# Causal scores of a chunk in pieces of 32 key columns, placed on the four column groups of TensorE

## The chip, the cores and the metric

The kernel runs on one core of one Trainium2 chip. The metric is the device time of one execution in microseconds (us); lower is better.

PE is the matmul array, PEld its weight loads, DVE the vector engine, ACT the scalar engine, POOL the GpSimd engine, SP the engine that issues most of the loads.

## The reference

Two blocks in sequence. The first is a gated linear recurrence over tokens (4 sequences, 8 heads, 768 tokens, 48 channels a head); the second a feed-forward layer on 3072 tokens of width 384, with 1024 hidden units.

```python
for t in range(S):                       # S = 768, for each of B = 4 sequences and H = 8 heads
    S_re, S_im = ar * S_re - ai * S_im, ar * S_im + ai * S_re
    S_re = S_re + einsum('bhd,bhe->bhde', k[:, :, t], v[:, :, t])
    y[:, :, t] = einsum('bhd,bhde->bhe', q[:, :, t], S_re)
x = y as (3072, 384)
h = x @ w_in                             # 384 -> 1024
solu = h * softmax(h)
out = layernorm(solu) * g_ln @ w_out     # 1024 -> 384
```

## The kernel before

The recurrence is computed in 24 chunks of 128 tokens. In a chunk each head needs scores (keys times queries, 128 x 128), of which only those with query token >= key token count; a mask of ones and zeros (`tri`) removes the rest. The masked scores (`f_att`) then weight the values (`f_v`), and the state carried from the chunks before is added. Everything is fp32.

```python
def score(half):                          # 4 heads each
    ps = ps_s.tile([P, 4, P], FP, tag="s", name="f_score")
    for i in range(4):
        x = half * 4 + i
        nc.tensor.matmul(out=ps[:, i], lhsT=KT[:, x * P:(x + 1) * P], rhs=QT[:, x * P:(x + 1) * P],
                         start=True, stop=True)
    nc.vector.tensor_tensor(out=st["att"][:, half * 4:half * 4 + 4], in0=ps,
                            in1=tri.unsqueeze(1).to_broadcast([P, 4, P]), op=OP.mult)

def values():
    V = T["v", g][:, own]
    ...
    for x in range(H):
        hs = slice(x * D, (x + 1) * D)
        for r in range(0, P, 32):         # four column groups: output partitions r..r+31
            nc.tensor.matmul(out=y[r:r + 32, hs], lhsT=st["att"][:, x, r:r + 32], rhs=V[:, hs], ...)
        ...                               # the same with qT and the carried state
```

The `values` step (`f_y`) and the carry (`f_d`, which updates the state) already use weights of 32 columns, written to output partitions 0, 32, 64 and 96, that is, to the four column groups of the array. The scores use all 128 columns at once. One iteration of the main loop, cut to the order that matters (the loop works on three chunks at a time, and every second iteration differs in the gate work):

```python
for n in range(2, N + 2):
    score(0); score(1)      # f_score of chunk n
    turn_x()                # f_xt: three 128-wide transposes of chunk n-1
    down(0)                 # f_o of chunk n-2
    values()                # f_y of chunk n
    up(0)                   # f_h of chunk n-1
    turn(...)               # f_turned: transposes of q and k of chunk n+1
    up(1)
    carry()                 # f_d of chunk n
    turn(...)
    down(1)
    turn_z(0); turn_z(1)    # f_zt of chunk n-1; in every second iteration f_phase follows
```

## Time and profile before

| what | value | where from |
|---|---|---|
| median time | 555.27 us (554.70 to 555.46, 3 runs) | the times |
| span of the profiled execution | 553.1 us | the page |
| third score starts (the loop begins) | 98.96 us | starts of matmuls in the trace |
| third score to the first matmul of the last f_o stage ("the loop" from here on) | 442.34 us | the same |
| mean granted PE clock, first 100 us / 100 to 500 us | 0.80 / 1.00 | busy time by windows |

The busy time of each engine, from the page:

```profile
PE 482.6 (87%) x5604; PEld 309.4 (56%) x5604; DVE 367.3 (66%) x714; ACT 305.4 (55%) x497; POOL 17.9 (3%) x52
```

87% for PE is an average over two regimes: the first 100 us, in which PE is often idle or slow, and a loop in which it hardly stops. The prediction below shows the lines for that. An fp32 matmul appears in the trace as two passes, each with a weight load of its own.

### The profile page before, as it was taken

The page shows a single profiled execution, that of the slowest core. Times are in us where ns is not written, and L with a number is a line of the kernel's source. Part 1 is how long each engine was busy: PE and PEld are TensorE (multiplying, and loading weights), DVE is VectorE, ACT ScalarE, POOL GpSimd, SP SyncE. Part 2 cuts the span into 40 slices and gives each one's busy share as a digit, 9 for nine tenths or more (in the row PEclk, how much of TensorE's full clock was granted, in tenths as well). Part 3 has the DMA queues.
Part 4 walks back from the last instruction along what each step waited for, and adds up shares of the span by engine and source line. Part 5 has one row for each costly group of instructions (what it writes and reads, how often), then busy time and mean ns, then how long its engine had stood idle before and what let it go on. Part 6 is the DMA issues. An engine that isn't in the chain of part 4 may idle for free. (4 is left out here: it accounts for less than half of the span.)

```text
span 553.1 us, 13053 instructions
## 1 busy us (share of the span) xinstructions
PE 482.6 (87%) x5604; PEld 309.4 (56%) x5604; DVE 367.3 (66%) x714; ACT 305.4 (55%) x497; POOL 17.9 (3%) x52
## 2 busy tenths in 40 slices
PE   0265744799999999999999999999999999999994
PEld 0144323455765666666666666567567656666652
DVE  4668435957677768759759669669578677564333
ACT  4755447375656565575575665665655665642220
POOL 0000000000000000000000000000000000000000
PEclk9957786899999999999999999999999999999999
DMA  9998633431613615416316305206214000000001
GB/s 205 235 246 159 129 97 104 109 66 39 115 54 59 130 44 88 102 44 115 75 44 131 58 17 101 58 17 120 44 32 82 14 3 17 14 17 1 15 15 36
DMA packets 134243, 42.23 MB, mean 76 GB/s; under 512 B 127392, under 2 KB 130464, under 8 KB 134176
## 3 DMA queue, kind: packets, MB, share of 16 engines
q1 hardware_dynamic: 133328, 40.91, 34.6%
q8 instruction: 46, 0.75, 0.6%
q10 hardware_dynamic: 848, 0.40, 0.3%
q14 instruction: 21, 0.17, 0.1%
HBM read 36.51 MB, written 4.72 MB: 75 GB/s over the span
## 5 line engine op out<-in xcount | busy, mean ns | idle before, releaser
L866 PE MATMUL f_h<-f_w_in,f_xT 128*128 128x512 f32 x288 | 135.7, 609 | 7.5 <-ACT f_xT L861 7.5
L908 PE MATMUL f_o<-f_w_out,f_zT 128*128 128x384 f32 x384 | 133.5, 492 | 2.5 <-DVE f_w_out L645 2.5
L908 PEld LDWEIGHTS f_o<-f_w_out,f_zT 128*128 128x128 f32 x384 | 70.2, 192 | 43.1 <-DVE f_w_out L645 2.7
L866 PEld LDWEIGHTS f_h<-f_w_in,f_xT 128*128 128x128 f32 x288 | 52.0, 193 | 57.7 <-issue 48.0
L874 ACT ACTIVATE f_z<-f_h 128x512 f32<-128x512 f32 x48 | 28.6, 597 | 91.5 <-PE f_h L866 91.5
L875 DVE TENSOR_TENSOR f_z<-f_h,f_z 128x512 f32<-128x512 f32 x48 | 33.1, 689 | 47.2 <-ACT f_z L874 47.2
L813 PEld LDWEIGHTS f_score<-f_qT,f_kT 96*128 96x128 f32 x384 | 46.5, 195 | 3.0
L813 PE MATMUL f_score<-f_qT,f_kT 96*128 96x128 f32 x384 | 47.6, 278 | 0.0
L796 PE MATMUL f_turned<-f_mats,f_k 128*96 128x128 f32 x192 | 32.1, 293 | 17.8 <-DVE f_k L784 17.8
L796 PEld LDWEIGHTS f_turned<-f_mats,f_k 128*96 128x96 f32 x192 | 21.8, 132 | 34.8 <-DVE f_k L784 25.3
L884 ACT COPY f_zT<-f_zt 128x512 f32<-128x512 f32 x48 | 26.7, 587 | 26.2 <-PE f_zt L883 25.6
L831 DVE COPY f_xn<-f_y 128x384 f32<-128x384 f32 x24 | 13.2, 552 | 41.6 <-PE f_y L828 35.4
L798 ACT COPY f_kT<-f_turned 96x512 f32<-96x512 f32 x48 | 27.6, 576 | 18.1 <-PE f_turned L796 18.1
L825 PEld LDWEIGHTS f_y<-f_v,f_att 128*32 128x32 f32 x1536 | 30.4, 109 | 8.9 <-issue 7.5
L703 PE MATMUL f_L<-f_lr,f_mats 128*128 128x384 f32 x48 | 19.0, 522 | 18.5 <-DVE f_lr L696 18.5
L825 PE MATMUL f_y<-f_v,f_att 128*32 128x48 f32 x1536 | 34.0, 207 | 0.3 <-DVE f_att L815 0.3
L815 DVE TENSOR_TENSOR f_att<-f_score,f_mats 128x512 f32<-128x512 f32 x48 | 31.1, 683 | 4.3 <-PE f_score L813 4.3
L796 PE MATMUL f_turned<-f_mats,f_q 128*96 128x128 f32 x192 | 31.3, 289 | 2.7 <-DVE f_q L784 2.7
L896 DVE BATCH_NORM_STATS2 f_bs<-f_z 128x6 f32<-128x512 f32 x48 | 30.7, 680 | 0.0
L704 DVE TENSOR_SCALAR f_lr<-f_L 128x384 f32<-128x384 f32 x24 | 13.3, 556 | 25.8 <-PE f_L L703 25.0
L828 PE MATMUL f_y<-f_state,f_qT 96*32 96x48 f32 x1280 | 29.8, 205 | 0.0
L798 ACT COPY f_qT<-f_turned 96x512 f32<-96x512 f32 x48 | 28.1, 585 | 2.9 <-PE f_turned L796 1.8
(98 smaller groups left out, 715.3 us busy)
## 6 DMA issues: line engine op xcount, KB each, us to landing
f_raw<-in_moe_w_in_dram SPq DMA_DIRECT2D x12, 512.0 KB, 5.4
f_raw<-in_moe_w_out_dram SPq DMA_DIRECT2D x16, 384.0 KB, 3.8
f_ar<-in_a_re_dram SPq DMA_DIRECT2D x24, 192.0 KB, 4.0
f_ai<-in_a_im_dram SPq DMA_DIRECT2D x24, 192.0 KB, 4.2
f_q<-in_q_dram SPq DMA_DIRECT2D x24, 192.0 KB, 4.6
f_k<-in_k_dram SPq DMA_DIRECT2D x24, 192.0 KB, 4.4
f_v<-in_v_dram SPq DMA_DIRECT2D x24, 192.0 KB, 4.4
out_dram<-f_ot SPq DMA_DIRECT2D x24, 192.0 KB, 2.1
```

The lines of the kernel that those rows point to most:

```text
L796: nc.tensor.transpose(out=ps[0:D2, i], in_=T[nm + "2", c][:, half * 4 + i].rearrange("p u d -> p (u d)"), identity=ident)
L798: nc.scalar.copy(out=T[nm + "T", c][:, half * 512:half * 512 + 512], in_=ps[0:D2].rearrange("p i t -> p (i t)"))
L813: nc.tensor.matmul(out=ps[:, i], lhsT=KT[:, x * P:(x + 1) * P], rhs=QT[:, x * P:(x + 1) * P], start=True, stop=True)
L815: nc.vector.tensor_tensor(out=st["att"][:, half * 4:half * 4 + 4], in0=ps, in1=tri.unsqueeze(1).to_broadcast([P, 4, P]), op=OP.mult)
L825: nc.tensor.matmul(out=y[r:r + 32, hs], lhsT=st["att"][:, x, r:r + 32], rhs=V[:, hs], start=True, stop=(ti == 0))
L828: nc.tensor.matmul(out=y[r:r + 32, hs], lhsT=T["qT", c][:, x * P + r:x * P + r + 32], rhs=state[b][:, hs], start=False, stop=True)
L866: nc.tensor.matmul(out=h, lhsT=st["xT"][:, c * P:(c + 1) * P], rhs=w_in[:, c, half * 512:(half + 1) * 512], start=(c == 0), stop=(c == KD ...
L874: nc.scalar.activation(out=z, in_=h, func=AF.Exp, accum_out=sums[:, ti * B + b, half:half + 1])
L875: nc.vector.tensor_tensor(out=z, in0=h, in1=z, op=OP.mult)
L884: nc.scalar.copy(out=st["zT"][:, half * 512:(half + 1) * 512], in_=ps)
L896: nc.vector.bn_stats(out=bs[:, i], in_=z[:, i * 512:(i + 1) * 512])
L908: nc.tensor.matmul(out=st["o"], lhsT=st["zT"][:, c * P:(c + 1) * P], rhs=w_out[:, c], start=(c == 0), stop=(c == KF - 1))
```

## The change

Intent: the mask throws away 192 of the 512 key-block-by-token columns of a head (blocks of 32 keys, tokens before the block). The change does not compute them. It cuts each head's keys into four blocks of 32 and multiplies each block only with the tokens from that block on: 128, 96, 64 and 32 moving columns. Each block goes to a column group of its own. In even heads block 0 (the longest) goes to group 0; in odd heads the order is reversed, so that every group gets 160 columns per pair of heads. Reversing the order permutes the rows of the odd heads' scores; hence a second mask `back` and a second copy of the odd heads' values with reversed blocks (`f_vr`), loaded by eight extra transfers of 24 KB for each group of two chunks. The score's two PSUM tiles become fixed and are cleared once, because the parts that are not written any more are still read by the mask product.

```diff
-    last = np.zeros((P, P))
-    last[P - 1] = 1.0
-    return np.concatenate([np.eye(P), tri, tri * (-0.5 / math.pi), last, np.ones((P, P))], 1).astype(np.float32)
+    back = tri.reshape(4, 32, P)[::-1].reshape(P, P)
+    return np.concatenate([np.eye(P), tri, back, tri * (-0.5 / math.pi), np.ones((P, P))], 1).astype(np.float32)
@@ load of a group
+            if nm == "v":
+                vr = T["vr", g] = ldv.tile([P, GB, H // 2, D], FP, tag="vr", name="f_vr")
+                for r in range(0, P, 32):
+                    t0 = ti * P + P - 32 - r
+                    for i in own:
+                        nc.sync.dma_start(out=vr[r:r + 32, i],
+                                          in_=v[b0 + i, 1::2, t0:t0 + 32, :].rearrange("h t d -> t h d"))
@@ score
-            ps = ps_s.tile([P, 4, P], FP, tag="s", name="f_score")
+            ps = scores[half]
             for i in range(4):
                 x = half * 4 + i
-                nc.tensor.matmul(out=ps[:, i], lhsT=KT[:, x * P:(x + 1) * P], rhs=QT[:, x * P:(x + 1) * P],
-                                 start=True, stop=True)
-            nc.vector.tensor_tensor(out=st["att"][:, half * 4:half * 4 + 4], in0=ps,
-                                    in1=tri.unsqueeze(1).to_broadcast([P, 4, P]), op=OP.mult)
+                for r in range(0, P, 32):
+                    r0 = P - 32 - r if i % 2 else r
+                    nc.tensor.matmul(out=ps[r0:r0 + 32, i, r:], lhsT=KT[:, x * P + r:x * P + r + 32],
+                                     rhs=QT[:, x * P + r:(x + 1) * P], start=True, stop=True)
+            nc.vector.tensor_tensor(
+                out=st["att"][:, half * 4:half * 4 + 4].rearrange("p (i u) t -> p i u t", u=2),
+                in0=ps.rearrange("p (i u) t -> p i u t", u=2),
+                in1=mats[:, 1:3].unsqueeze(1).to_broadcast([P, 2, 2, P]), op=OP.mult
+            )
@@ values
+                rhs = T["vr", g][:, own, x // 2] if x % 2 else V[:, hs]
-                    nc.tensor.matmul(out=y[r:r + 32, hs], lhsT=st["att"][:, x, r:r + 32], rhs=V[:, hs], start=True,
+                    nc.tensor.matmul(out=y[r:r + 32, hs], lhsT=st["att"][:, x, r:r + 32], rhs=rhs, start=True,
@@ start (cut: the two fixed score tiles are declared above)
+    for t in scores:
+        nc.vector.memset(t, 0.0)
```

More of the change, by code (lines that the diff above doesn't have):

```diff
@@ L549, in whole @@
     ps_t = pool("f_ps_t", 2, space=PSUM)
-    ps_s = pool("f_ps_s", 2, space=PSUM)
+    ps_s = pool("f_ps_s", 1, space=PSUM)
     ps_y = pool("f_ps_y", 1, space=PSUM)
@@ L555, in whole @@
     mats = const.tile([P, 5, P], FP, name="f_mats")
-    ident, tri, turns, last, ones = (mats[:, i] for i in range(5))
+    ident, tri, _, turns, ones = (mats[:, i] for i in range(5))
     bias = const.tile([P, 6], FP, name="f_bias")
@@ L573, in whole @@
     T = {}
+    scores = [ps_s.tile([P, 4, P], FP, tag=f"s{i}", name=f"f_score{i}") for i in range(2)]
     def heads(t):
```

## The prediction

> **What bounds the kernel now.** I read the page's busy row by slices first, then the groups by cost, the waits of the PE in the middle of the run, and last the timeline of single iterations. From the page:
>
> ```profile
> span 553.1 us, 13053 instructions
> ...
> PE   0265744799999999999999999999999999999994
> PEld 0144323455765666666666666567567656666652
> DVE  4668435957677768759759669669578677564333
> ACT  4755447375656565575575665665655665642220
> ```
>
> From slice 8 (about 100 us) to slice 38 the PE row stands at 9 and no other engine does. The first seven slices are another regime: weight conversion and the first gates on DVE and ACT, PE cold and waiting. The waits of the PE between 140 and 520 us confirm it; this is the whole answer:
>
> ```profile
> PE f_phase L756 <- DVE f_x L746: 2.6, 9, 0.3
> PE f_turned L796 <- DVE f_q L784: 2.1, 9, 0.2
> ```
>
> 4.7 us of waits in 380 us: the time there is the sum of what the PE streams. Scores (L813) are made once for each of 24 blocks of 128 tokens (a chunk). Their start times in the trace run from 38.0 to 512.9 us; the third starts at 99.0, so **22 of the 24 lie in the PE-bound stretch**. Two groups matter:
>
> ```profile
> L813 PE MATMUL f_score<-f_qT,f_kT 96*128 96x128 f32 x384 | 47.6, 278 | 0.0
> ...
> L825 PE MATMUL f_y<-f_v,f_att 128*32 128x48 f32 x1536 | 34.0, 207 | 0.3 <-DVE f_att L815 0.3
> ```
>
> x384 is 24 chunks x 8 heads x 2: each fp32 matmul appears as two passes with a weight load each. The mean of 278 ns is latency and not rate; for the rate I use starts in the PE timeline of one chunk (start, length, what):
>
> ```profile
> 321.76 1.95 PE L813 MATMUL f_score<-f_qT,f_kT 96*128 96x128 f32 x16
> 323.55 0.49 PE L858 MATMUL f_xt<-f_mats,f_xn 128*128 128x128 f32 x3
> 323.88 2.75 PE L908 MATMUL f_o<-f_w_out,f_zT 128*128 128x384 f32 x8
> 326.56 0.29 PE L825 MATMUL f_y<-f_v,f_att 128*32 128x48 f32 x8
> ...
> 328.09 2.84 PE L866 MATMUL f_h<-f_w_in,f_xT 128*128 128x512 f32 x6
> ...
> 336.44 2.75 PE L908 MATMUL f_o<-f_w_out,f_zT 128*128 128x384 f32 x8
> 339.02 1.04 PE L883 MATMUL f_zt<-f_mats,f_z 128*128 128x128 f32 x8
> ```
>
> The score occupies 323.55 - 321.76 = **1.79 us**, 112 ns a pass. That is 128 moving columns at 0.833 ns (106.7 ns; f_o: 2.58 us / 8 / 384 columns = 0.84 ns) and 5 ns more, since the equally long load of 128 weight columns sits beside each pass.
>
> **What the Trainium skill says.** (1) "TensorE: Matmul & The Clock Gate", Part 3: an output at PSUM partitions 32j puts a 32-wide matmul on column group j, and such matmuls run concurrently. The values step already does this: the timeline shows 8 passes of f_y of 48 columns every 87 ns, so 4 passes every 43.5 ns, of which streaming 48 columns is 40 ns. All four groups stream at once, with 3.5 ns lost a pass. The same part says that matmuls start strictly in program order. The trace does not agree: the two passes of a matmul follow each other in the program on the same group, yet first passes of all four groups start 7 ns apart (305.289 to 305.309 us) and second passes after them (from 305.356). Each group thus behaves as its own queue, on which the change relies. (2) "TensorEngine Tiling (Array Packing)", Key Properties: "Mode switching requires drain". The trace agrees and gives the size: f_o to f_y takes 326.56 - 323.88 = 2.68 us where f_o to f_zt takes 2.58, about 0.09 us exactly (416 against 323 ns from last start to first start); leaving f_y, the last start comes 133 ns before the next stage, 0.09 more than one pass. (3) Same TensorE page, LDWEIGHTS section: load time goes with the weight columns. Agrees: 110 ns latency for 32 columns against 192 for 128. (4) "PSUM — Partial Sum Buffer", bank collisions: different column tiles may write one bank together. f_y already writes one bank from four groups.
>
> **The change part by part.** *Removed:* 16 passes of 128 columns a chunk, 1.787 us.
>
> *Added:* 32 matmuls = 64 passes, with 128, 96, 64 and 32 columns. A key block on the diagonal is only needed from its own tokens on, so 320 of 512 head-columns are streamed. If every head put its 128-column piece on group 0, group 0 would still stream 8 x 2 x 128 columns: 8 x 2 x (106.7 + 3) = 1.76 us, nothing gained. With odd heads reversed each group gets 128 + 32 or 96 + 64 columns in a pair of heads: 2 x (160 x 0.833 + 2 x 3) = 279 ns, four pairs **1.115 us**. The 3 ns is my choice between 3.5 (f_y) and 2.7 (f_d, 42.7 ns a pass). To this: 27 ns until the first weights are in (the first f_y pass lasts 230 ns and not 206) and about 20 ns of stagger. An in-order dispatch with a few passes queued a group, followed by hand over the sequence, gives 1.14 to 1.17 us; I take 1.16.
>
> *Added by mode:* before, score lay between 128-wide transposes, at no cost. Now it needs a switch in and one out, 2 x 0.093 = 0.19 us.
>
> So 1.16 + 0.19 = 1.35 us against 1.79: **0.44 us saved a chunk**. Times 22: **9.6 us**.
>
> *Moved on DVE:* the mask product keeps its elements (128x512, 683 ns) and reads two masks instead of one: no change. Two memsets of 128x512 in PSUM at the start (estimate, from 512 elements at the product's 1.33 ns: 0.7 us each) fall into the 5.08 us in which DVE waits for the first f_ar: free.
>
> *Added DMA:* for each of 12 groups 8 transfers of 24 KB with the odd heads' values in reversed blocks, 96 issues and 2.4 MB on top of 173 and 42.2 MB. The last f_v is issued at 415 us and used after 490; loads run far ahead. In the loop they are hidden. At the start the DMA row is full[...], so I expect 3 to 5 us of delay for what follows the first group's values; f_ar for the second group is issued at 18.6 us and used at 41.2, weights issued at 27.3 are used at 52.5: inside the slack.
>
> *Added on PE's sequencer:* the odd heads wait for up to four more semaphores; one such wait takes 51 ns. It runs about 32 instructions ahead of the array, which is 0.17 us in f_y, so 4 x 51 = 204 ns may not be hidden wholly. I take off 0.03 us a chunk: 0.7 us. Against it, the first score at half clock ends some 0.4 us sooner, on the DVE chain of the start. Sum: 9.6 - 0.7 + 0.4 = **9.3 us, 555.3 to 546.0**.
>
> **The rivals.** *A wait in place of the work.* Values need the masked scores. DVE's timeline:
>
> ```profile
> 323.66 1.28 DVE L815 TENSOR_TENSOR f_att<-f_score,f_mats 128x512 f32<-128x512 f32 x2
> ...
> 342.77 1.28 DVE L815 TENSOR_TENSOR f_att<-f_score,f_mats 128x512 f32<-128x512 f32 x2
> ```
>
> The first ends at 324.94, 1.6 us before f_y. The second belongs to the iterations in which DVE has been busy without a break since 331.7; it ends at 344.05 and f_y starts at 344.84: 0.79 us of slack, of which the change eats 0.44. It holds, barely. If DVE is slower than I think, half the chunks gain less: 11 x 0.2 = 2 us lost, 548.
>
> *Column groups do not overlap with unequal lengths.* If dispatch blocked at the head of the line, a head would last at least its 128-column piece: no gain and 0.19 us of switches, 22 x 0.2 = 4 us lost, 559. Against it: the order of starts in f_y. For it: f_y shows equal lengths only. I give it 6%.
>
> *Switches cost less,* or overlap with the stage before, or passes are at 2.5 ns overhead: 0.5 us a chunk, 11 us, 544. Against: the 93 ns stood the same in each of 13 entries.
>
> *Transfers at the start* push a critical load: 1 to 4 us worse. Early waits of ACT and DVE for DMA sum to some 8 us, all on loads issued before the new ones, which speaks against it.
>
> **Range and chances.** 2% is 11.1 us, or 0.5 us a chunk: just beyond the sum. So within 2% is likeliest. An 8-in-10 range of 542.5 to 551; faster by over 2% (below 544.2) 0.18, slower 0.05, the rest within.
>
> **What would show each step.** Score's first start to f_xt's first start should fall from 1.79 to about 1.26 us, with about 0.09 more between f_zt or f_phase and score. In the groups, L813 should become x1536 with four shapes. The waits of the PE should stay at a few us with no new one on f_att above 2 us, and none on f_vr. The third score should start within 1 us of 99.0; if it starts later, transfers at the start are the cause. The prediction is wrong if the score stays above 1.5 us (groups not concurrent), if f_y waits for f_att, or if the time before 100 us grows by more than 2 us.

## The result, and the profile after

The changed kernel's median is 546.17 us (545.41 to 547.09, 4 runs), against 555.37 us (554.70 to 555.55, 4 runs) of the kernel before in the same rounds. The ratio is 0.9837, with a 95% interval of 0.9817 to 0.9858. A ratio here is the mean time of one kernel's runs over the mean of the other's of the same rounds, so it is not quite the ratio of the medians. Executions over 1.5% slower than the fastest of the same kernel are left out of the means. All outputs are right. The gain, 1.6%, is real and lies within the 2% that counts as the same.

The page of the changed kernel:

```profile
span 543.6 us, 15486 instructions
...
PE 472.0 (87%) x6756; PEld 293.1 (54%) x6756; DVE 368.1 (68%) x716; ACT 305.7 (56%) x497; POOL 17.9 (3%) x52
...
PE   0264745699999999999999999999999999999994
```

PE stands at 9 from slice 8 on, as before. Its instructions went from 5604 to 6756, and its busy time fell by 10.6 us. The waits of the PE between 140 and 510 us show the same two lines with the same numbers, so no new wait took the place of the work:

```profile
PE f_phase L766 <- DVE f_x L756: 2.6, 9, 0.3
PE f_turned L806 <- DVE f_q L794: 2.1, 9, 0.2
```

The groups of PE instructions by form (line, engine, operation, out<-in, shape, count, then busy us and mean ns of one):

```profile
L827 PE MATMUL f_score<-f_qT,f_kT 96*32 96x128 f32 x384 | 32.0, 276 | 0.0
L827 PE MATMUL f_score<-f_qT,f_kT 96*32 96x96 f32 x384 | 31.2, 248 | 0.0
L827 PE MATMUL f_score<-f_qT,f_kT 96*32 96x32 f32 x384 | 31.0, 196 | 0.0
L827 PE MATMUL f_score<-f_qT,f_kT 96*32 96x64 f32 x384 | 30.9, 220 | 0.0
```

The four shapes appear 384 times each. Each is busy for 31 to 32 us, and the whole group has one busy time of 32.0 us, not the sum: all four shapes run over the same stretches of time. How long one stretch is, the PE timeline of one chunk shows (start, length, engine, line, what, count):

```profile
315.62 1.13 PE L766 MATMUL f_phase<-f_x,f_mats 128*128 128x384 f32 x3
316.69 1.33 PE L827 MATMUL f_score<-f_qT,f_kT 96*32 96x128 f32 x64
317.95 0.55 PE L876 MATMUL f_xt<-f_mats,f_xn 128*128 128x128 f32 x3
```

Read starts, not lengths: the score's first pass to the first f_xt takes 317.95 - 316.69 = 1.26 us, where it took 1.79 us before. That is 0.52 us a chunk and would be 11.5 us over 22 chunks. The whole gain is smaller, so something was given back. To find it I split the loop, from the third score to the first matmul of the last f_o stage, by stage, taking for each stage the time from its first start to the next stage's first start (all from starts of matmuls in the trace of one profiled execution each, 22 chunks, us):

| stage | before | after | difference |
|---|---|---|---|
| f_score | 39.30 | 27.83 | -11.47 |
| f_xt (just after f_score) | 10.31 | 11.87 | +1.56 |
| f_zt (ahead of f_score in half of the iterations) | 28.98 | 29.99 | +1.01 |
| f_phase (ahead of f_score in the other half) | 13.65 | 14.59 | +0.94 |
| f_y | 32.25 | 32.51 | +0.26 |
| the whole loop | 442.34 | 434.66 | -7.68 |

The stages not listed did not change. f_zt and f_phase pay the entry into the 32-column mode: from their last start to the first score takes 203 ns where it took 109, and 416 where it took 323, that is 93 to 94 ns. f_xt pays after the exit: from the start of its first pass to the start of its second takes 165 ns and not 113, 52 ns in each chunk, 1.1 us in all. The trace shows where they go: the second pass's weight load starts 55 ns after the first pass (318.005 us against 317.950), where before the change it started with it (323.552 against 323.551). The same 165 ns stand, in both kernels, between the first two passes of f_zt behind f_L, where PE waited for DVE and changed no mode; so this part goes with a PE that had stopped, and not with the switch alone. The other 0.4 us of f_xt is one wait for a weight in the third chunk. The exit's drain itself lies inside the 1.26 us: from the last score pass to f_xt takes 149 ns where it took 112.

Of the rest of the two profiled executions' difference, 0.2 us lies behind the loop and 1.6 us ahead of it: the third score starts at 97.36 us and not 98.96. DVE's timeline of the first chunk, before:

```profile
39.73 0.69 DVE L815 TENSOR_TENSOR f_att<-f_score,f_mats 128x512 f32<-128x512 f32 x1 [1.48 <-PE f_score L813]
40.62 0.69 DVE L815 TENSOR_TENSOR f_att<-f_score,f_mats 128x512 f32<-128x512 f32 x1 [0.20 <-PE f_score L813]
41.23 0.94 DVE L660 TENSOR_SCALAR_CACHE_REDUCE f_ar<-f_ar 128x768 f32<-128x768 f32 x1
```

and after:

```profile
38.58 1.29 DVE L829 TENSOR_TENSOR f_att<-f_score,f_mats 128x512 f32<-128x512 f32 x2 [0.58 <-PE f_score L827]
39.78 0.94 DVE L670 TENSOR_SCALAR_CACHE_REDUCE f_ar<-f_ar 128x768 f32<-128x768 f32 x1
```

The brackets hold DVE's idle time before the instruction and what ended it. Here DVE waits for the scores, 1.48 + 0.20 us before and 0.58 us after, and goes on to the next gates (f_ar) at 39.78 us and not 41.23. In this one place the faster score frees DVE, which is busy ahead of the loop. The granted clock has a part in it: the first score took 2.55 us from its first start to the next stage before and 1.60 us after (both with the wait that follows it), a part of the former at half clock.

### The profile page after: what moved, and what is told of

It reads as the page before. It is cut to its first block, busy times and chain, and to the rows that moved or that the text cites. A ratio compares the mean times of both kernels' runs of the same rounds, so it can differ in the third digit from the quotient of the medians.

```text
span 543.6 us, 15486 instructions
## 1 busy us (share of the span) xinstructions
PE 472.0 (87%) x6756; PEld 293.1 (54%) x6756; DVE 368.1 (68%) x716; ACT 305.7 (56%) x497; POOL 17.9 (3%) x52
## 5 line engine op out<-in xcount | busy, mean ns | idle before, releaser
L827 PEld LDWEIGHTS f_score<-f_qT,f_kT 96*32 96x32 f32 x1536 | 28.8, 110 | 8.0 <-issue 8.0
L827 PE MATMUL f_score<-f_qT,f_kT 96*32 96x96 f32 (+3 forms) x1536 | 32.0, 235 | 0.0
L901 PEld LDWEIGHTS f_zt<-f_mats,f_z 128*128 128x128 f32 x192 | 21.5, 141 | 13.2 <-DVE f_lr L714 8.5
L901 PE MATMUL f_zt<-f_mats,f_z 128*128 128x128 f32 x192 | 27.9, 279 | 0.2
```

The costliest lines, as they stand in the source:

```text
L827: nc.tensor.matmul(out=ps[r0:r0 + 32, i, r:], lhsT=KT[:, x * P + r:x * P + r + 32], rhs=QT[:, x * P + r:(x + 1) * P], start=True, stop=True)
L901: nc.tensor.transpose(out=ps[:, i * P:(i + 1) * P], in_=st["z"][:, c * P:(c + 1) * P], identity=ident)
```

## The experiments

The theory: **each column group works through its own sequence of passes, and the fullest group sets the stage's time; in return every stretch of 32-column work pays for a switch in and a switch out.** From it follow four things that its rivals deny: fewer columns alone are worth nothing, without the switches the balance is worth more, coarser pieces cost by the columns of the fullest group, and 22 of 24 parts of the gain lie in the loop. Ten kernels ran, on three chips, each batch with its own runs of the kernel before (medians 555.78, 555.31 and 555.60 us). The texts on record give theories and rivals letters; I name them in words.

### Skip the columns, but do not balance them

```diff
-    back = tri.reshape(4, 32, P)[::-1].reshape(P, P)
+    back = tri
-                    t0 = ti * P + P - 32 - r
+                    t0 = ti * P + r
-                    r0 = P - 32 - r if i % 2 else r
+                    r0 = r
```

> The change without the reversal: all heads put their 128-column piece on column group 0, masks and values in natural order, the extra value loads kept. Theory A (each column group is a queue of its own, and the fullest group sets the time): group 0 streams 8 x 2 x (106.7 + 3) ns = 1.76 us a chunk, so score to f_xt takes about 1.88 us (27 ns first weights, 20 ns stagger, 94 ns drain) against 1.265 with the reversal and 1.787 before; with 0.093 us at entry and 0.055 us in the first f_xt pass it is slower than the kernel before by 22 x 0.24 = 5 us: about 561 us. Rival B (what counts is the number of columns streamed in all, 37% fewer): as fast as with the reversal, 546 us.

Measured: median 560.94 us (559.71 to 561.32), ratio to the kernel before 1.0094 (1.0076 to 1.0111). One chunk in the PE timeline:

```profile
302.61 1.04 PE L901 MATMUL f_zt<-f_mats,f_z 128*128 128x128 f32 x8
303.57 1.94 PE L827 MATMUL f_score<-f_qT,f_kT 96*32 96x128 f32 x64
305.44 0.55 PE L876 MATMUL f_xt<-f_mats,f_xn 128*128 128x128 f32 x3
```

The same 64 passes with the same column counts as in the changed kernel take 305.44 - 303.57 = 1.87 us instead of 1.26. Group 0 always has the 128-column piece, and eight heads x two passes of 128 columns at 0.833 ns are 1.71 us, whatever the other groups do. The 37.5% of columns that the change skips are worth nothing until they are spread evenly.

### Neither skip nor balance: four full pieces

This is the kernel before, with its masks and loads, and only the score matmul cut:

```diff
-                nc.tensor.matmul(out=ps[:, i], lhsT=KT[:, x * P:(x + 1) * P], rhs=QT[:, x * P:(x + 1) * P],
-                                 start=True, stop=True)
+                for r in range(0, P, 32):
+                    nc.tensor.matmul(out=ps[r:r + 32, i], lhsT=KT[:, x * P + r:x * P + r + 32],
+                                     rhs=QT[:, x * P:(x + 1) * P], start=True, stop=True)
```

> The kernel before with each score matmul cut into four pieces of 32 weight columns, each over all 128 tokens; no reversal, no extra loads. Theory A: every group streams 8 x 2 x 128 columns, the same 1.76 us as group 0 in the natural-order run, so the same 1.88 us from score to f_xt and about 561 us: the pure price of the two mode switches a chunk, since the streaming is unchanged. Rival C (the short pieces gain by themselves, as the load of 128 weight columns goes away): faster than 555 us. Skipping columns without balance is then worth nothing if this run and the natural-order run agree within 2 us.

Measured: 560.24 us (559.87 to 561.24), ratio 1.0082 (1.0066 to 1.0097).

```profile
303.89 1.95 PE L814 MATMUL f_score<-f_qT,f_kT 96*32 96x128 f32 x64
305.78 0.55 PE L859 MATMUL f_xt<-f_mats,f_xn 128*128 128x128 f32 x3
```

1.89 us with all columns, against 1.87 us with 37.5% of them left out: the same within 20 ns, so unbalanced skipping and no skipping cost the same. Both kernels' loops are longer than before by 5 us (447.21 and 447.41 us against 442.34). This kernel has none of the extra loads and none of the new masks, so the 5 us over 22 chunks, 0.23 us each, are the price of going to 32-column pieces and back. It consists of the entry (0.093), the longer stretch, with the exit's drain in it (1.885 - 1.786 = 0.099), and the first f_xt pass, with 165 ns to the second in this kernel too (+0.052): 0.24 us, close to what the loop shows. Here the last pass of every group has 128 columns, as before the change, so the drain can be read directly: from the last score pass to f_xt takes 203 ns and not 112, 0.091 us. The penalty on f_xt thus belongs to the switch and not to what the change put into it.

### Pieces of 64

```diff
-                for r in range(0, P, 32):
-                    r0 = P - 32 - r if i % 2 else r
-                    nc.tensor.matmul(out=ps[r0:r0 + 32, i, r:], lhsT=KT[:, x * P + r:x * P + r + 32],
+                for r in range(0, P, 64):
+                    r0 = P - 64 - r if i % 2 else r
+                    nc.tensor.matmul(out=ps[r0:r0 + 64, i, r:], lhsT=KT[:, x * P + r:x * P + r + 64],
```

(The second mask and the reversed values are cut into blocks of 64 in the same way, with half as many extra loads.)

> The change with pieces of 64 weight columns in place of 32: two pieces of 128 and 64 tokens a head, odd heads' two key blocks exchanged. Theory A: each half of the array streams 192 columns in a pair of heads, 4 x 2 x (160 + 6) ns = 1.33 us, about 1.50 us from score to f_xt against 1.265: 22 x 0.235 = 5 us slower than the change, 551 us, and 4 us faster than before. Rival D (the number of passes sets the pace, 32 against 64 a chunk): faster than the change, under 545 us.

Measured: 552.45 us (551.45 to 554.12), ratio 0.9949 (0.9928 to 0.9971).

```profile
298.39 1.56 PE L827 MATMUL f_score<-f_qT,f_kT 96*64 96x128 f32 x32
299.89 0.55 PE L876 MATMUL f_xt<-f_mats,f_xn 128*128 128x128 f32 x3
```

1.50 us in this chunk, against 1.26 with pieces of 32. In a pair of heads each half now streams 128 + 64 = 192 columns in place of 160: 32 columns x 2 passes x 4 pairs x 0.833 ns = 0.213 us, and the medians over the chunks differ by 1.492 - 1.265 = 0.227 us. The loop is 4.5 us longer than the change's (439.19 against 434.66). Twice as many instructions cost less than 20% more columns: the number of pieces is not what bounds the stage, the columns of a group are.

### Share one switch between two stages

The carry (`f_d`) is the other 32-column stage with 128-wide neighbours on both sides. Its result, the state, is needed only when the same sequence comes up again. Here it moves directly ahead of the next chunk's scores, so both share one entry and one exit:

```diff
+    late_carry = lambda: None
     for n in range(2, N + 2):
...
         if n < N:
+            late_carry()
             score(0)
             score(1)
+            late_carry = carry
...
-        if n < N:
-            carry()
```

> The change, with the 32-column matmuls of the state update (f_d) of one chunk moved to stand directly before the scores of the next, so that the array stays in one mode through both. Theory A with its switch price: 18 chunks each save the entry into the scores (0.093 us) and the exit from f_d (0.094 us and 0.041 us in the first pass after it), 18 x 0.228 = 4.1 us: 542 us, 0.75% under the change. Rival E (VectorE has under 0.4 us of slack before the values in every second chunk; the state update now stands right before the mask product and the values wait): no gain, 546 us or more, with waits of f_y for f_att.

Measured: 543.84 us (541.81 to 544.22), ratio 0.9779 (0.9761 to 0.9796): **faster than the kernel before by over 2%**.

```profile
294.60 1.04 PE L901 MATMUL f_zt<-f_mats,f_z 128*128 128x128 f32 x8
295.56 0.84 PE L858 MATMUL f_d<-f_v,f_k 128*32 128x48 f32 x45
296.20 0.22 PE L827 MATMUL f_score<-f_qT,f_kT 96*32 96x32 f32 x1
296.22 0.22 PE L858 MATMUL f_d<-f_v,f_k 128*32 128x48 f32 x3
296.25 1.30 PE L827 MATMUL f_score<-f_qT,f_kT 96*32 96x32 f32 x63
297.49 0.55 PE L876 MATMUL f_xt<-f_mats,f_xn 128*128 128x128 f32 x3
```

There is no drain between f_d and the score: the first score pass, the 32-column piece of head 0, starts at 296.20 us, ahead of the last three passes of f_d (from 296.22), which stand before it in the program. It belongs to group 3, and f_d, with an output of 96 partitions, uses groups 0 to 2 only. That is the theory's "each group has its own sequence" seen directly. The stretch from the first score pass to f_xt is 1.29 us (297.49 - 296.20; 1.265 in the changed kernel), and the loop falls from 434.66 to 430.20 us, by 4.46 us. Only 18 of the 22 chunks have a carry joined to them, so that is 0.25 us for each, where 0.228 was expected for one entry, one exit and one slow first pass. The rival, a new wait in place of the switch (for f_att or for the state), fell: the waits of the PE in the loop did not change. f_y alone takes 0.6 us more over the loop: 67 ns more in about half of the chunks, against four of them in the changed kernel. The time of the whole missed the expected 542 us by 1.8 us, and not in the loop: the third score came at 100.66 us, 3.3 us later than in the changed kernel (see "The extra loads alone").

### Where the start's microsecond comes from

Three kernels and a repeat of the change ran together. `again` is the changed kernel once more. `late` uses the new scores in the 22 loop chunks and the old ones in the first two; `early` is its mirror image (`if c > 1`).

```diff
+                if c < 2:
+                    nc.tensor.matmul(out=ps[:, i], lhsT=KT[:, x * P:(x + 1) * P], rhs=QT[:, x * P:(x + 1) * P],
+                                     start=True, stop=True)
+                    continue
...
+                in1=(tri.unsqueeze(1).unsqueeze(1).to_broadcast([P, 2, 2, P]) if c < 2
+                     else mats[:, 1:3].unsqueeze(1).to_broadcast([P, 2, 2, P])), op=OP.mult
...
-                rhs = T["vr", g][:, own, x // 2] if x % 2 else V[:, hs]
+                rhs = T["vr", g][:, own, x // 2] if x % 2 and c > 1 else V[:, hs]
```

> The changed kernel once more, on the chip of the runs beside it. From its trace: the part from the third score to the last matmul shrank by 7.7 us (22 x 0.36 with the first-pass cost after the switch), and the part before the third score by 1.6 us, of which I trust only the 0.9 us by which the first score is shorter. If the start's gain was chance of the clock windows (W), 547.5 to 548; if it is real (S), 546 again.

> The old scores in the first two chunks, the new ones in the 22 others. The loop's gain alone: 555.6 - 7.7 = 547.9 us if the start's gain is real (S), that is 1.0 to 1.5 us slower than the changed kernel; equal to the changed kernel within 0.5 us if it is not (W).

> The new scores in the first two chunks alone, the old ones in the 22 others; all extra loads and memsets kept. Theory S (in the start the half-clocked first score is on the way: second mask product at 39.19 us against 40.62): 1.0 to 1.5 us faster than the kernel before, about 554.3. Rival W (the difference of the starts is where the clock's windows of 3.4 us fall): no difference beyond 0.5 us, 555.4.

| kernel | median (range), us | ratio to before (95%) | loop, us | third score, us |
|---|---|---|---|---|
| again | 546.75 (545.54 to 548.09) | 0.9847 (0.9833 to 0.9861) | 434.65 | 97.44 |
| late | 548.00 (546.42 to 548.60) | 0.9870 (0.9856 to 0.9884) | 434.72 | 98.16 |
| early | 554.77 (554.30 to 557.05) | 0.9989 (0.9976 to 1.0002) | 442.04 | 101.54 |

The repeat reproduces the change, in its loop within 0.01 us. `late` keeps the whole loop gain (434.72 us), so the loop gain comes from the 22 chunks alone. It loses 1.25 us of median against `again`; `early` gains 0.5 us of median over the kernel before, with an interval that includes no gain at all. If the start's gain was real, 1.0 to 1.5 us were expected of both; `late` fits that, `early` does not, and single executions of the repeat spread over 2.5 us. Both point to a gain of 0.5 to 1.3 us from the first two chunks, not to a sure number.

### The extra loads alone

The kernel before, with the extra transfers in natural order, and the odd heads' values read from them:

```diff
+            if nm == "v":
+                vr = T["vr", g] = ldv.tile([P, GB, H // 2, D], FP, tag="vr", name="f_vr")
+                for r in range(0, P, 32):
+                    t0 = ti * P + r
+                    for i in own:
+                        nc.sync.dma_start(out=vr[r:r + 32, i],
+                                          in_=v[b0 + i, 1::2, t0:t0 + 32, :].rearrange("h t d -> t h d"))
...
+                rhs = T["vr", g][:, own, x // 2] if x % 2 else V[:, hs]
```

> The kernel before with the extra loads alone (96 transfers, 2.4 MB) and with odd heads' values read from them, in natural order; scores untouched. Theory A: the loads are hidden, and the extra waits on PE's sequencer cost 22 x 0.01 us: 555.4 to 556.2. Rival D (the loads delay what the start waits for): 557 to 559, the third score later than 101 us, waits for f_ar or f_raw.

Measured: 556.08 us (554.78 to 556.58, 6 runs), ratio 1.0004 (0.9992 to 1.0017). On the mean the loads cost nothing that five rounds can see. The profiled execution of this kernel nevertheless has a wait that the kernel before has not: ACT is idle for 1.8 us near 85 us. The same stands in the profiles of `early` (2.3 us) and of the kernel with the joined carry, where ACT's timeline reads:

```profile
84.59 0.83 ACT L720 ACTIVATE f_ar<-f_lr 128x768 f32<-128x768 f32 x1
87.23 0.52 ACTq L722 DMA_DIRECT2D f_ends<-f_ar  x1
87.79 0.64 ACT L626 ACTIVATE f_bits<-f_raw,f_bias 128x384 f32<-128x384 uint32 x1 [2.37 <-DMA f_on<-f_f]
```

against the changed kernel's:

```profile
83.02 0.83 ACT L720 ACTIVATE f_ar<-f_lr 128x768 f32<-128x768 f32 x1
83.88 0.52 ACTq L722 DMA_DIRECT2D f_ends<-f_ar  x1
84.45 0.63 ACT L626 ACTIVATE f_bits<-f_raw,f_bias 128x384 f32<-128x384 uint32 x1 [0.60 <-ACT f_ar L720]
```

ACT is ready to issue the small store `f_ends` at about 85.4 us, and issues it at 87.23, when an earlier small transfer (`f_on`, 3 KB) has landed. In these programs the two count on the same semaphore. The idle time in the brackets holds the issue itself, 0.60 us in the changed kernel, which did not wait; the wait proper is 1.8 us here, 1.7 in `early` and 1.3 in `loads`. (The 0.7 us of `natural`, which a text below counts too, are hardly a wait: 0.1 us.) The transfers of that stretch, 78 to 90 us, show what f_on shared it with (size each, and median us from issue to landing); with the joined carry:

```profile
f_raw<-in_moe_w_in_dram SPq DMA_DIRECT2D x3, 512.0 KB, 5.3
f_vr<-in_v_dram SPq DMA_DIRECT2D x5, 24.0 KB, 2.0
f_on<-f_f ACTq DMA_DIRECT2D x1, 3.0 KB, 6.3
```

and in the changed kernel:

```profile
f_raw<-in_moe_w_in_dram SPq DMA_DIRECT2D x4, 512.0 KB, 4.3
...
f_on<-f_f ACTq DMA_DIRECT2D x1, 3.0 KB, 1.6
```

The 3 KB of f_on need 6.3 us in the one and 1.6 us in the other. In both, the weights (f_raw, 512 KB each) are loaded in this stretch; before the change they were issued earlier, at 67.6 and 72.0 us, and the eight extra issues of a group, each about 0.45 us on SP, pushed them back. Whether f_on meets them is a matter of a few microseconds, and all twelve profiles agree on it: f_on takes 4.5 to 6.3 us in the four (joined carry, `loads`, `early`, `natural`) in which it is issued within 1.4 us after the first weights of this stretch, at 80.89 after 80.5 us with the joined carry, and 1.6 to 2.3 us in the eight in which it is issued ahead of them, at 79.32 before 80.7 us in the changed kernel, or 3 us and more after those before it.

### Fewer, larger extra loads

If those waits cost time, half as many issues should help. The extra loads of a group are made in four transfers of 48 KB, once in the changed kernel (`merged`) and once with the joined carry as well (`joined_merged`):

```diff
-                    for i in own:
-                        nc.sync.dma_start(out=vr[r:r + 32, i],
-                                          in_=v[b0 + i, 1::2, t0:t0 + 32, :].rearrange("h t d -> t h d"))
+                    nc.sync.dma_start(out=vr[r:r + 32].rearrange("p b h d -> p (b h) d"),
+                                      in_=vf[b0 * H + 1:(b0 + GB) * H:2, t0:t0 + 32, :].rearrange("h t d -> t h d"))
```

(`vf` is `v` with its first two axes merged.)

> The change with the eight extra loads of a group joined into four of twice the size (same bytes). In five of the executions profiled so far ACT waited 0.7 to 2.4 us near 85 us for the landing of its own small transfer f_on, which shares a completion counter with f_ends and lies behind large weight loads that the extra issues had pushed to 80 us; in the other profiles of kernels with the extra loads it did not. Here SyncE issues 1.8 us less a group and the two small transfers have separate counters. Theory L (that wait is what spreads the times of the changed kernel from 545.4 to 548.1): near the lower end in all rounds, 545.5 to 546.2, no such wait in the profile. Rival W (the clock's windows spread them): median 546.7 and a spread of 2 us as before.

> Both: state-update matmuls directly before the next scores, and four extra loads a group. Loop 430.2 us as measured in the joined run. Theory L: 541.5 to 542.2, under the 543.8 of the joined run, which had the 2.4 us wait in its profile. Rival W: 543.8 again.

Measured: `merged` 546.73 us (546.09 to 548.16), ratio 0.9839 (0.9826 to 0.9853), which is the changed kernel's own ratio: nothing gained. The recorded theory, 545.5 to 546.2 us without the wait, fell here, and its rival, 546.7, fits. `joined_merged` 541.04 us (540.83 to 542.61), ratio **0.9745** (0.9732 to 0.9758), 2.8 us of median below the kernel with the joined carry alone (of another batch), and the fastest. The wait is absent from both profiles, and f_on and f_ends count on separate semaphores in both. The loop of `joined_merged` (429.87 us) agrees with the joined kernel's (430.20), so its gain lies mostly in the start: the third score is at 98.31 us and not 100.66. Of those 2.35 us the wait proper is 1.8, and about 0.6 stood there ahead of it: ACT's f_ar starts at 83.95 us and not 84.59. This points to the wait as the larger part there, in one profile of each. In the changed kernel it can't be what fewer loads would mend: neither of its two profiles (the first and `again`) has the wait.

What else moves the start is the clock. The granted clock by slices (tenths of full speed, a slice is a fortieth of the span), the changed kernel first, then `merged`:

```profile
PEclk9997786899999999999999999999999999999999
```

```profile
PEclk9978686899999999999999999999999999999999
```

From the third slice on the two differ although the work is the same; the trace shows windows at half clock whose lengths are multiples of 3.41 us, and they fall differently in each execution. Over the first 100 us the mean was 0.80 in the profile before, 0.86 in the one after, 0.83 in `merged` and 0.81 in `joined_merged`. The third score started between 97.4 and 101.5 us over all twelve profiled executions, and neither the clock nor the ACT wait alone puts them in order. I have one profile a kernel, so how a start divides into the two stays open.

## Why the prediction was right or wrong

The predicted time was 546.0 us and the measured median 546.17. The total is right, but that it is right within 0.2 us is luck: two of its terms were off in opposite directions and cancelled.

- **PE-bound loop, 22 chunks: right.** `late` has the whole loop gain; the waits of the PE did not change in any kernel where I looked (before, after, unbalanced, four full pieces, pieces of 64, both with the joined carry).
- **Each group as its own queue, balance needed: right.** Unbalanced pieces took 1.87 us and full ones 1.89, where the prediction's sum for group 0 gave 1.76 before the exit. The rival of head-of-line blocking fell.
- **Score stretch of 1.26 us, entry of 0.09 us: right.** 1.265 and 0.093 to 0.094 us.
- **What the switch out costs: the term that was mis-sized.** The prediction took 0.093 us for the exit, from the drain alone, and overlooked that the second pass after it starts late, because its weights do: 165 ns after the first, against 113. The view was there before the change: the first f_turned pass after f_d took 150 ns to the next and not 109, the first f_h pass after f_y 533 and not 429. I measured the drain on the 32-column stage's last pass and never looked at the first pass of the stage behind it. Cost: 0.052 us a chunk, 1.1 us in all.
- **Waits for semaphores on PE's sequencer, 0.7 us: smaller.** Nothing shows there but f_y's 0.26 us, 67 ns in each of four chunks. `loads`, with the extra loads and the old scores, shows the same four; the four full pieces, without those loads, show none. The loop therefore gained 7.7 us where 8.9 was predicted, the 0.4 us wait for a weight in the third chunk included.
- **The start, 0.4 us: too small in the profiled execution, and not settled.** It gave 1.6 us there, outside the 1 us that the prediction allowed the third score; the experiments say 0.5 to 1.3, on top of variation between executions. The prediction counted the shorter matmuls at half clock. It did not count that DVE, which waits for both halves, then goes straight on to the next gates, so that its time is the start's too: there it was 1.45 us earlier.
- **Loads hidden: right in the mean, wrong in one detail.** `loads` has a ratio of 1.0004. But the prediction looked for the delay in what follows the *first* group's values, and it appears near 85 us, on ACT, through a small transfer behind large ones; some kernels have it and others not.
- **DVE's slack of 0.79 us holds: right.** No wait of PE for f_att appeared in the loop.
- **One reading goes too far, without weight in the sum.** The prediction sees the time of a weight load go with its columns, 110 ns for 32 and 192 for 128. But the loads of f_zt and f_xt have 128 columns too and last 140 and 143 ns in the same trace, so something besides the columns counts; no run here shows what.

## What to carry to other kernels

When a masked product is cut into column tiles, count the columns of the fullest tile and not the sum: the skipped work is worth something only once the tiles are even, here by reversing every second head. Charge each stretch of narrow tiles for a switch in, a switch out and a slow first pass behind it (0.23 us together here), and put narrow stages next to each other: moving one already narrow stage gave 4.5 us, more than half of what the change's new arithmetic gave in the loop. A total that comes out right is no proof of its terms; split it by stage before believing it.

## What the Trainium skill lacked or had wrong

- "TensorE: Matmul & The Clock Gate", Part 3, says that matmuls start and end strictly in program order. Here the starts do not across column groups: with the joined carry a score pass starts at 296.20 us, ahead of three f_d passes from 296.22 us that precede it in the program. Nor does the page say that tiles of unequal length must be balanced by group: 1.87 us unbalanced against 1.26 us balanced for the same passes.
- "TensorEngine Tiling (Array Packing)", Key Properties, says that a mode switch drains TensorE, with which the traces agree, but gives no size. Here: 0.093 us in, 0.091 us out (four full pieces), and 0.04 to 0.10 us more in the first pass after it (52 ns on f_xt, 41 on f_turned, 104 on f_h). Sharing one switch pair between two stages saved 0.25 us in each of 18 chunks.
- "DMA: Bandwidth & Descriptors", section "Why a DMA increments its semaphore by 16 and not by 1", asks for one semaphore per transfer in flight for the sake of correctness. It does not mention the price in time: an issue that waited 1.8 us for a 3 KB transfer which shared its semaphore and took 6.3 us instead of 1.6.
- "TensorE: Matmul & The Clock Gate", Part 1, gives the clock window of 3.41 us, and the traces agree (half-clock stretches in multiples of it). The page says too that the slow start varies from run to run, but gives no figure for the comparison of two programs with a long slow start: here, over the first 100 us, the mean granted clock was 0.80 to 0.88 in twelve profiled executions with nearly the same work, and the five executions of the repeated kernel spread over 2.5 us. How much of that spread is the clock's is open.
